# A decode layer on one NeuronCore: the order of the first loads, the cut of the last one, and the block around the programs

Three small edits were made at once to a kernel that is already bound by its loads. The last 64 rows of the q weights are loaded before the other 512. The block that wrapped the programs of the five engines is gone. The last chunk of `W_down` arrives in four pieces of 3, 3, 2 and 1 rows instead of three of 6, 2 and 1.

## Chip, cores and metric

The kernel runs on one core of a Trainium2 chip. The metric is the device time of one execution in microseconds (us). Each execution also has a *span*: the time from the first to the last instruction that the trace shows.

## The reference

It is one transformer layer at decode time (batch 4, one token, width 576):

```python
h  = x + attention(layernorm(x))      # 32 heads, 16 kv heads, head size 128, last 4096 cache positions
h2 = h + mlp(layernorm(h))            # relu(x W_gate) * (x W_up), then W_down [4608, 576]
```

The cache window and the weights are some 160 MB in bf16, each byte used once.

## The kernel before

The kernel writes lists of operations, one list per engine, with dependencies by name. `emit` turns these into semaphore waits. The parts that the change touches, cut:

```python
    def emit(self, nc, es):
        # ... number the operations, make the semaphores ...
        block = es.enter_context(nc.Block())
        def run(engine, e):
            # ... for each operation: wait for its dependencies, issue it, signal ...
        for e in ENGS:
            getattr(block, e)(lambda engine, e=e: run(engine, e))
```

In the trace of this kernel, at the line that closes the block, SyncE branches at 378.2 us, and all five engines drain and meet in a barrier whose semaphore records run from 378.39 to the end of the span at 378.58.

All large loads go through SyncE's queue, in order: q weights, then K and V tiles of 4 MB through four slots, then `A_wo`, `W_gate`, `W_up` and `W_down`:

```python
        place(("wq", 0), wq_off, TILE, "QMM", ...)        # 512 rows, 128 x 32 KB
        P.dma("sync", ("L", "wq", 1), ...)                # 64 rows, 128 x 4 KB
        # ... K and V tiles, then the other weights ...
        for j in range(4):                                # W_down: 4 chunks of 9 rows per partition
            for r0, r1 in ((0, 9),) if j < 3 else ((0, 6), (6, 8), (8, 9)):
                place(("wd", j, r0), ...)
```

The last stage multiplies each row of `W_down` (two matmuls, `n` = 0 and 1) as its piece lands. Then both halves are copied out of PSUM, the output is stored, and SyncE waits for the store to land:

```python
        for j in range(4):
            for r in range(9):
                for n in range(2):
                    if n == 0:
                        if r == 0 or (j == 3 and r in (6, 8)):
                            deps.append(("L", "wd", j, r))
                    pe(("DOWN", n), ...)
        # ... two copies, two stores ...
        P.op("sync", None, None, [("O", n) for n in range(2)])
```

## Time and profile before

| what | value |
|---|---|
| time before the prediction, 3 runs | median 380.56 us (379.36 to 380.57) |
| time of the profiled run, and its span | 380.66 us, 378.58 us |
| bytes loaded, mean rate over the span | 159.7 MB, 422 GB/s |

Four lines of the page of the kernel before follow: PE and the other engines with busy time, share and instruction count; the DMA engines' busy tenths in 40 slices of the span; and the chain of work that ended last, by engine and by line.

```profile
PE 213.2 (56%) x1471; PEld 37.6 (10%) x703; DVE 225.6 (60%) x164; ACT 54.4 (14%) x85; POOL 10.6 (3%) x29
...
DMA  8999999999999999999999999999999999999994
...
DMA 56%; PE 22%; DVE 20%; issue 0%; SPq 0%; ACT 0%
DMA sb_arena<-in_A_k_cache_dram 48%; DVE sb_arena L427 16%; PE psb L34 13%; DMA sb_arena<-in_B_W_down_dram 8%; PE psb L451 4%; PE psb L512 3%; DVE sb_o_tmp L525 1%; DVE sb_pp L490 1%; PE psb L707 1%; PE psb L478 1%; DVE sb_pp L473 0%; DVE sb_hx L456 0%; ACT sb_pp L470 0%; SPq L286 0%; DVE sb_out_sb L710 0%
```

The DMA engines are busy from the second slice to the last but one, and no compute engine is busy more than 60%. The chain is mostly waits for loads. So only the two ends can be gained from, unless the rate changes.

The end of the chain of waits, in order of time (start, duration, what):

```profile
341.77 32.17 DMA sb_arena<-in_B_W_down_dram
373.94 0.04 issue
373.98 2.39 PE psb L707 x18
376.37 0.43 DVE sb_out_sb L710
```

The timeline of the same stretch shows start, duration, engine, line, operation and shape; in brackets stand the idle time before and what ended it:

```profile
371.93 1.28 PE L707 MATMUL psb<-sb_arena,sb_pp 128*32 128x288 bf16 x18 [1.83 <-DMA sb_arena<-in_B_W_down_dram]
...
373.98 2.35 PE L707 MATMUL psb<-sb_arena,sb_pp 128*32 128x288 bf16 x18 [0.77 <-DMA sb_arena<-in_B_W_down_dram]
376.36 0.45 DVE L710 CAST sb_out_sb<-psb 32x288 bf16<-32x288 f32 x1 [10.68 <-PE psb L707]
```

And the same stretch by windows: length, busy time of PE, PEld (weight loads), DVE, ACT and POOL with instructions in brackets, then the granted PE clock (1.00 is full speed), the DMA share and GB/s:

```profile
371.00:373.30 2.30, 1.28 (x18) 0.82 (x18) 0.00 (x0) 0.00 (x0) 0.00 (x0) 1.00 0.82 333
373.30:374.00 0.70, 0.02 (x2) 0.02 (x4) 0.00 (x0) 0.00 (x0) 0.00 (x0) 0.54 0.46 171
374.00:375.00 1.00, 1.00 (x10) 0.67 (x12) 0.00 (x0) 0.00 (x0) 0.00 (x0) 0.50 0.08 30
375.00:376.40 1.40, 1.33 (x12) 0.54 (x8) 0.04 (x1) 0.01 (x1) 0.00 (x0) 0.50 0.00 0
```

Each of the two matmul groups has 18 matmuls of the same shape. The first took 1.28 us, the second 2.35 us. The window view gives the reason: the clock granted to PE is 1.00 up to 373.3 and 0.50 from 374 on.

The end of the execution, by line: what SyncE's sequencer did on the block's closing line (its count, minimum, median and maximum in ns, first and last start in us):

```profile
L136 SPq COMPARE_BRANCH  x1: 33/33/33, 378.2 to 378.2; - x1
L136 SPq DRAIN  x1: 7/7/7, 378.4 to 378.4; - x1
L136 SPq EVENT_SEMAPHORE  x1: 17/17/17, 378.5 to 378.5; - x1
```

The output had landed at 378.18 by the record of landings. The branch, the drain and the barrier that follow end the span at 378.58.

### The profile page before, as it was taken

The numbers are of one execution on the slowest core, as the hardware profiler recorded it, in microseconds if no ns is written. First come the engines' busy times: TensorE is split into PE (matmuls) and PEld (weight loads), VectorE is DVE, ScalarE is ACT, GpSimd is POOL, SyncE is SP. The second block draws the span as 40 slices with busy tenths as digits, with TensorE's granted clock in tenths as the row PEclk, the third lists the DMA queues.
The fourth block names the chain that finished last, engine by engine and source line by source line (L and its number), as shares of the span: only waits on it lengthen the run. The fifth ranks groups of instructions, "written<-read, shape, count | busy, mean of one in ns | idle before, by whom it ended". The sixth has DMA issues, their size and how long they took to land.

```text
span 378.6 us, 2587 instructions
## 1 busy us (share of the span) xinstructions
PE 213.2 (56%) x1471; PEld 37.6 (10%) x703; DVE 225.6 (60%) x164; ACT 54.4 (14%) x85; POOL 10.6 (3%) x29
## 2 busy tenths in 40 slices
PE   0404442239919091749292835573746697885764
PEld 0000000001001010101010100010100011002422
DVE  3178878779392959593848777666658513334120
ACT  3192000211010114010101140101010501113010
POOL 8200000000000000000000000000000000000000
PEclk9966866659969788697888796989686978998697
DMA  8999999999999999999999999999999999999994
GB/s 333 440 443 429 409 435 443 443 429 409 435 443 440 427 414 433 443 436 426 419 435 443 429 426 426 435 433 436 429 422 435 436 429 429 448 413 421 418 423 183
DMA packets 6659, 159.74 MB, mean 422 GB/s; under 512 B 749, under 2 KB 889, under 8 KB 1529
## 3 DMA queue, kind: packets, MB, share of 16 engines
q1 hardware_dynamic: 6632, 159.59, 98.3%
q8 instruction: 8, 0.13, 0.1%
q14 instruction: 3, 0.02, 0.0%
q10 hardware_dynamic: 16, 0.01, 0.0%
HBM read 159.58 MB, written 0.00 MB: 422 GB/s over the span
## 4 chain that ended last, share of the span: by engine, by line
DMA 56%; PE 22%; DVE 20%; issue 0%; SPq 0%; ACT 0%
DMA sb_arena<-in_A_k_cache_dram 48%; DVE sb_arena L427 16%; PE psb L34 13%; DMA sb_arena<-in_B_W_down_dram 8%; PE psb L451 4%; PE psb L512 3%; DVE sb_o_tmp L525 1%; DVE sb_pp L490 1%; PE psb L707 1%; PE psb L478 1%; DVE sb_pp L473 0%; DVE sb_hx L456 0%; ACT sb_pp L470 0%; SPq L286 0%; DVE sb_out_sb L710 0%
## 5 line engine op out<-in xcount | busy, mean ns | idle before, releaser
L427 DVE STREAM_TRANSPOSE sb_arena<-sb_arena 128x8192 f32<-128x8192 f32 (+1 forms) x19 | 139.9, 7365 | 67.5 <-DMA sb_arena<-in_A_k_cache_dram 67.5
L451 PE MATMUL psb<-sb_arena 128*32 128x512 bf16 x256 | 41.8, 627 | 120.3 <-DVE sb_arena L427 120.3
L34 PE MATMUL psb<-sb_arena,sb_pp 128*128 128x512 bf16 x384 | 108.3, 392 | 0.0
L512 PE MATMUL psb<-sb_arena,sb_pp 128*128 128x512 bf16 x128 | 50.9, 398 | 8.9 <-DVE sb_o_tmp L525 8.9
L522 ACT COPY sb_o_tmp<-psb 32x512 f32<-32x512 f32 x32 | 18.5, 578 | 181.4 <-PE psb L34 181.1
L34 PE MATMUL psb<-sb_arena 128*32 128x512 bf16 x256 | 43.4, 645 | 0.0
L525 DVE TENSOR_TENSOR sb_o_tmp<-psb,sb_fm 32x512 f32<-32x512 f32 x32 | 21.7, 678 | 18.6 <-PE psb L34 18.1
L451 PEld LDWEIGHTS psb<-sb_arena 128*32 128x32 bf16 x256 | 9.1, 119 | 162.9 <-DVE sb_arena L427 133.3
L512 PEld LDWEIGHTS psb<-sb_arena,sb_pp 128*128 128x128 bf16 x128 | 12.8, 100 | 116.6 <-issue 116.6
L529 DVE TENSOR_REDUCE sb_o_sel<-sb_o_tmp 128x128 f32<-128x512 f32 x16 | 17.7, 1105 | 0.5
L470 ACT ACTIVATE sb_pp<-psb,sb_hx 128x1024 bf16<-128x1024 f32 x4 | 4.5, 1114 | 80.7 <-DVE sb_hx L467 80.7
L490 DVE TENSOR_TENSOR sb_pp<-psb,sb_m 128x1024 bf16<-128x1024 f32 x8 | 9.3, 1207 | 4.8 <-PE psb L478 4.8
L485 ACT ACTIVATE sb_pp<-psb,sb_m 128x512 bf16<-128x512 f32 x16 | 9.7, 693 | 14.9 <-PE psb L478 14.9
L528 DVE TENSOR_TENSOR sb_o_tmp<-sb_o_tmp,sb_fm 64x512 f32<-64x512 f32 x16 | 11.0, 689 | 0.5
L418 ACT COPY sb_arena<-sb_q_keep 32x256 bf16<-32x256 bf16 x8 | 9.7, 1449 | 0.1
L707 PE MATMUL psb<-sb_arena,sb_pp 128*32 128x288 bf16 x72 | 6.2, 327 | 4.0 <-DMA sb_arena<-in_B_W_down_dram 4.0
L473 DVE STREAM_TRANSPOSE sb_pp<-sb_pp 128x1024 bf16<-128x1024 bf16 x4 | 5.0, 1245 | 5.1 <-ACT sb_pp L470 5.1
L478 PE MATMUL psb<-sb_pp,sb_to_v 128*32 128x256 bf16 x64 | 4.3, 401 | 6.3 <-DVE sb_pp L473 6.3
L404 DVE CAST sb_pp<-psb 128x512 bf16<-128x512 f32 x1 | 2.4, 2427 | 8.8 <-PE psb L384 8.8
L710 DVE CAST sb_out_sb<-psb 32x288 bf16<-32x288 f32 x1 | 0.4, 446 | 10.7 <-PE psb L707 10.7
L34 PE MATMUL psb<-sb_arena,sb_hnT 128*32 128x384 bf16 x80 | 6.4, 405 | 0.0
L456 DVE TENSOR_REDUCE sb_hx<-psb 128x1 f32<-128x1024 f32 x4 | 4.9, 1225 | 2.0 <-PE psb L34 2.0
(123 smaller groups left out, 81.2 us busy)
## 6 DMA issues: line engine op xcount, KB each, us to landing
sb_arena<-in_A_k_cache_dram SPq DMA_DIRECT2D x16, 4096.0 KB, 26.2
sb_arena<-in_A_v_cache_dram SPq DMA_DIRECT2D x16, 4096.0 KB, 28.5
sb_arena<-in_A_wo_dram SPq DMA_DIRECT2D x1, 4608.0 KB, 25.0
sb_arena<-in_B_W_gate_dram SPq DMA_DIRECT2D x1, 4608.0 KB, 26.5
sb_arena<-in_A_wq_dram SPq DMA_DIRECT2D x1, 4096.0 KB, 12.4
sb_arena<-in_B_W_down_dram SPq DMA_DIRECT2D x3, 1296.0 KB, 30.6
sb_arena<-in_B_W_up_dram SPq DMA_DIRECT2D x1, 3456.0 KB, 27.5
sb_arena<-in_B_W_up_dram SPq DMA_DIRECT2D x1, 1152.0 KB, 29.9
```

The costliest lines, as they stand in the source:

```text
L34: return e.add_instruction(mybir.InstMatmult(name=e.bass.get_next_instruction_name(), engine=mybir.EngineType.PE, ins=[e.lower_ap(rhs), e. ...
L418: act("QW", lambda e, i=i, q=q: e.copy(out=bass.AP(tensor=arena, offset=32 * i * AW + 2 * i + q, ap=[[AW, 32], [512, 16], [136, 4], [32, 4]]),
L427: dve(("TRA", g), lambda e: e.transpose(out=dst, in_=src), [("L", "K", g)] if lo == 0 else [])
L451: fn = lambda e, out_=out_, lhsT=lhsT, rhs=rhs, start=start, stop=stop: e.matmul(out_, lhsT=lhsT, rhs=rhs, start=start, stop=stop, skip_gr ...
L485: act(("EV", b, 0), lambda e, a=a: e.activation(out=bass.AP(tensor=pp, offset=2 * a, ap=[[PPW, 128], [8, 2], [32, 128], [1, 2]]), in_=bank ...
L490: dve(("EV", b, 1), lambda e, n=n: e.tensor_tensor(out=bass.AP(tensor=pp, offset=16 + 8 * n, ap=[[PPW, 128], [32, 128], [2, 4], [1, 2]]), ...
L512: fn = lambda e, lhsT=lhsT, rhs=rhs, k=k, j=j: e.matmul(bank[2 + j], lhsT=lhsT, rhs=rhs, start=(k == 0), stop=(k == 7), skip_group_check=True)
L522: act(("OSC", g), lambda e, j=j: e.copy(out=o_tmp[32 * j:32 * j + 32, 0:512], in_=bank[2 + j][32 * j:32 * j + 32, :]), [("PV", g), ("OSEL" ...
L525: dve(("OSD", g), lambda e, j=j: e.tensor_tensor(out=ot(32 * j, 32), in0=bank[2 + j][32 * j:32 * j + 32, :].rearrange("p (t d) -> p t d", ...
L528: dve(("OS", g), lambda e: e.tensor_tensor(out=ot(64, 64), in0=ot(64, 64), in1=fmb(64, 64), op=ALU.mult), [("OSC", g)])
L529: dve(("OSEL", g), lambda e: e.tensor_reduce(out=o_sel[:, qd, b, :], in_=o_tmp[:, 0:512].rearrange("p (t d) -> p d t", d=DH), axis=AX.X, o ...
L707: pe(("DOWN", n), lambda e, j=j, r=r, n=n, wv=wv: e.matmul(bank[n][32 * n:32 * n + 32, 0:288], lhsT=hhT[:, r * 128 + 32 * j:r * 128 + 32 * ...
```

## The change

The intent: SyncE's first load becomes the short one, the branches and the closing barrier go away, and PE has less to do after the last large piece has landed. Where the text speaks of 4 KB or 32 KB runs, it means the contiguous bytes that a load brings to one partition, not runs of the kernel.

```diff
-        block = es.enter_context(nc.Block())
-
@@
         for e in ENGS:
-            getattr(block, e)(lambda engine, e=e: run(engine, e))
+            run(getattr(nc, e), e)
@@
+        P.dma("sync", ("L", "wq", 1), lambda e: e.dma_start(out=pT[:, 0:2048], in_=last_rows(A_wq)), "d_wq1")
         s = ring_slot()
         wq_off = slot0 + s * TILE
         place(("wq", 0), wq_off, TILE, "QMM", ...)
-        P.dma("sync", ("L", "wq", 1), lambda e: e.dma_start(out=pT[:, 0:2048], in_=last_rows(A_wq)), "d_wq1")
@@
-            for r0, r1 in ((0, 9),) if j < 3 else ((0, 6), (6, 8), (8, 9)):
+            for r0, r1 in ((0, 9),) if j < 3 else ((0, 3), (3, 6), (6, 8), (8, 9)):
@@
-                        if r == 0 or (j == 3 and r in (6, 8)):
+                        if r == 0 or (j == 3 and r in (3, 6, 8)):
```

## The prediction

> **What bounds the kernel now.** One stream of loads. The page's slice table shows the DMA engines at 9 tenths from the second slice to the last but one, 422 GB/s over the span (159.7 MB, 378.6 us). The chain that ended last is 56% DMA; in order of time it ends "341.77 32.17 DMA W_down", 2.39 us of matmuls, a 0.43 us copy. PE (56% busy) and DVE (60%) do not set the pace. Only the start and the tail after the last bytes can pay; the rate between is left alone.
>
> **Parts of the change.**
>
> 1. W_down in 3, 3, 2, 1. By the records of landings the piece of 6 rows lands at 373.94, the next at 374.70, the last at 375.01. The timeline shows chunk 2's 18 matmuls from 371.93 in 1.28 us (done 373.2), PE idle until 373.98, then 18 matmuls in 2.35 us: the window table grants clock 0.50 from 374 on, so a row (2 matmuls) costs 0.24 us instead of 0.13. When row 6 is reached its data is there: the tail after 373.98 is PE work, not DMA. The 6 rows landed 2.05 us after chunk 2 (371.89), so 3 rows should land near 372.95 (estimate), and PE does them in its gap, from 373.2. Rows 3 to 5 start near 374.0; rows 6 (landing about 374.8) and 8 (about 375.1) hold nothing up. Three rows fewer after 374: 0.72 us[...]: **-0.65 us**. At full clock only about -0.1: then the landing at 375.0 binds.
>
> 2. No block. After the output lands (378.18) the records show wait and branch at 378.20, a drain, and a barrier of all engines ending at 378.58: **-0.35 us** if nothing replaces it. At the start one branch per engine goes between release (0.73) and first issue (0.80): at most **-0.05**.
>
> 3. Last 64 rows of the q weights first. K tile 0 still lands at 24.21. The 4 MB part lands near 14.5 instead of 13.24; q matmuls begin 1.25 us later and the query matrix is written near 27.3 instead of 26.0. Its reader waits for the transpose of K tile 0 (24.24 + 8.72 = 32.96): 5.6 us of slack. The next K load waits for the q matmuls (issue 17.8, then 19), with loads queued to 43.6. So 0. The first packets are 4 KB instead of 32 KB; the ramp may move by ±0.2.
>
> **Sum.** -0.65 - 0.35 - 0.05 = -1.05 us on 380.56: **379.5 us**, range **378.5 to 380.6** (the runs before span 1.2 us). Faster by over 2%: 0.01; within 2%: 0.985; slower by over 2%: 0.005.
>
> **What would show it.** Of the last 18 matmuls 6 before 373.9, the last 0.65 earlier; last landing up to 0.1 later. No drain and barrier after the output lands. The q matmuls at 14.5, K tile 0's transpose still at 24.2.
>
> **What would make it wrong.** The stream's end is set by the slowest of 16 DMA engines: the last piece's completions run from 372.63 to 375.01[...]. [...] So would another clock grant in the tail.

The sum came to -1.05 us. Cut are passages that no trace or run here shows: in part 1 an allowance that took its 0.72 us to the -0.65 of the sum, and in the last paragraph a reason for the spread of the completions and one further way in which the stream's end might move. "So would another clock grant" means: it too would move the end. The "±0.2" of the ramp and "up to 0.1 later" were my allowances, not measured: later, over all profiles, K tile 0's first completion came 0.27 us earlier with the order changed, and the last landing 0.38 earlier.

## More of the kernel before

The span is shorter than the time, and the difference turns out to matter here. I call it "time minus span".

All runs quoted are of the state that the measurements call fast. Within that state a second grouping shows up: of 64 runs of the kernel before, 43 took 379.33 to 379.78 us and 21 took 380.24 to 380.73 us, with none between. I call them *usual* and *long* runs.

## The result and the profile after

In the measurement of the pair, the changed kernel took 377.88 us (median of 6 runs, 377.84 to 378.10) and the kernel before 379.69 (6 runs, 379.36 to 380.57). The ratio is 0.9948, with a 95% interval of 0.9935 to 0.9961. A ratio here is the mean time of one kernel's fast runs over that of the other's of the same rounds, so it is not quite the ratio of these medians. By the means the gain is 1.97 us (377.92 against 379.90), by usual runs 1.64 us (377.88 against 379.52, the median of all 43 usual runs; the later gains in usual runs are against this too). I had forecast 1.05.

The page after, the same lines as before:

```profile
PE 208.8 (55%) x1456; PEld 37.6 (10%) x703; DVE 226.2 (60%) x164; ACT 54.3 (14%) x85; POOL 10.5 (3%) x29
...
DMA  8999999999999999999999999999999999999996
...
DMA 56%; PE 21%; DVE 20%; issue 1%; SPq 1%; ACT 0%
DMA sb_arena<-in_A_k_cache_dram 48%; DVE sb_arena L425 16%; PE psb L34 13%; DMA sb_arena<-in_B_W_down_dram 9%; PE psb L449 4%; PE psb L510 3%; DVE sb_o_tmp L523 1%; DVE sb_pp L488 1%; PE psb L476 1%; SPq L284 0%; DVE sb_pp L471 0%; DVE sb_hx L454 0%; ACT sb_pp L468 0%; PE psb L705 0%; DVE sb_out_sb L708 0%
```

The shares are the same: the kernel is still one stream of loads. The end of the chain, the timeline, the windows, and the line on which SyncE now ends, as before:

```profile
341.69 32.31 DMA sb_arena<-in_B_W_down_dram
374.00 0.04 issue
374.04 0.70 PE psb L705 x6
374.74 0.43 DVE sb_out_sb L708
```

```profile
371.23 1.65 PE L705 MATMUL psb<-sb_arena,sb_pp 128*32 128x288 bf16 x24 [1.82 <-DMA sb_arena<-in_B_W_down_dram]
...
373.33 0.55 PE L705 MATMUL psb<-sb_arena,sb_pp 128*32 128x288 bf16 x6 [0.46 <-DMA sb_arena<-in_B_W_down_dram]
...
374.04 0.66 PE L705 MATMUL psb<-sb_arena,sb_pp 128*32 128x288 bf16 x6 [0.17 <-DMA sb_arena<-in_B_W_down_dram]
374.73 0.45 DVE L708 CAST sb_out_sb<-psb 32x288 bf16<-32x288 f32 x1 [9.73 <-PE psb L705]
```

```profile
371.00:373.30 2.30, 1.65 (x24) 1.09 (x24) 0.00 (x0) 0.00 (x0) 0.00 (x0) 1.00 0.87 345
373.30:374.00 0.70, 0.55 (x6) 0.21 (x6) 0.00 (x0) 0.00 (x0) 0.00 (x0) 1.00 0.42 152
374.00:375.00 1.00, 0.66 (x6) 0.21 (x6) 0.27 (x1) 0.24 (x1) 0.00 (x0) 1.00 0.00 0
375.00:376.40 1.40, 0.00 (x0) 0.00 (x0) 0.18 (x1) 0.15 (x1) 0.00 (x0) 1.00 0.01 3
```

```profile
L110 SPq EVENT_SEMAPHORE  x1: 17/17/17, 376.6 to 376.6; - x1
```

The group at 371.23 holds 24 matmuls: the 18 of chunk 2 and the 6 of rows 0 to 2 of the last chunk, done in PE's former gap. Rows 3 to 5 follow at 373.33, and the last six matmuls at 374.04, each piece's as it lands. The clock is 1.00 throughout. After the output's landing (376.55) there is one wait of SyncE and nothing else. The output's own way, from the copy to its landing, is unchanged (1.82 us in both).

Part by part, the two profiles and times differ so (before, after):

| term | before | after | difference |
|---|---|---|---|
| last piece of `W_down` landed | 375.01 | 374.35 | -0.66 |
| from there to the start of the copy (376.36, 374.73) | 1.35 | 0.38 | -0.97 |
| output landed to end of span | 0.40 | 0.03 | -0.37 |
| time minus span | 2.08 | 1.28 | -0.80 |

The last row is not in the span at all, so no view of the profile shows it. The sum is -2.8 us, more than the gain by means or by usual runs: the profiled run of before, at 380.66, was a long one. These four terms are what the experiments had to sort out.

### The profile page after: what moved, and what is told of

The parts are those of the page before. It is cut to its first block, busy times and chain, and to the rows that moved or that the text cites. A ratio compares the mean times of both kernels' runs of the same rounds, so it can differ in the third digit from the quotient of the medians.

```text
span 376.6 us, 2562 instructions
## 1 busy us (share of the span) xinstructions
PE 208.8 (55%) x1456; PEld 37.6 (10%) x703; DVE 226.2 (60%) x164; ACT 54.3 (14%) x85; POOL 10.5 (3%) x29
## 4 chain that ended last, share of the span: by engine, by line
DMA 56%; PE 21%; DVE 20%; issue 1%; SPq 1%; ACT 0%
DMA sb_arena<-in_A_k_cache_dram 48%; DVE sb_arena L425 16%; PE psb L34 13%; DMA sb_arena<-in_B_W_down_dram 9%; PE psb L449 4%; PE psb L510 3%; DVE sb_o_tmp L523 1%; DVE sb_pp L488 1%; PE psb L476 1%; SPq L284 0%; DVE sb_pp L471 0%; DVE sb_hx L454 0%; ACT sb_pp L468 0%; PE psb L705 0%; DVE sb_out_sb L708 0%
## 5 line engine op out<-in xcount | busy, mean ns | idle before, releaser
L449 PE MATMUL psb<-sb_arena 128*32 128x512 bf16 x256 | 44.5, 640 | 118.8 <-DVE sb_arena L425 118.8
L34 PE MATMUL psb<-sb_arena,sb_pp 128*128 128x512 bf16 x382 | 107.3, 389 | 2.9 <-issue 2.8
L510 PE MATMUL psb<-sb_arena,sb_pp 128*128 128x512 bf16 x115 | 44.8, 389 | 8.9 <-DVE sb_o_tmp L523 8.9
L34 PE MATMUL psb<-sb_arena 128*32 128x512 bf16 x256 | 45.4, 645 | 0.0
L705 PE MATMUL psb<-sb_arena,sb_pp 128*32 128x288 bf16 x72 | 5.4, 288 | 3.8 <-DMA sb_arena<-in_B_W_down_dram 3.8
```

Source lines behind the costliest of these rows:

```text
L34: return e.add_instruction(mybir.InstMatmult(name=e.bass.get_next_instruction_name(), engine=mybir.EngineType.PE, ins=[e.lower_ap(rhs), e. ...
L449: fn = lambda e, out_=out_, lhsT=lhsT, rhs=rhs, start=start, stop=stop: e.matmul(out_, lhsT=lhsT, rhs=rhs, start=start, stop=stop, skip_gr ...
L510: fn = lambda e, lhsT=lhsT, rhs=rhs, k=k, j=j: e.matmul(bank[2 + j], lhsT=lhsT, rhs=rhs, start=(k == 0), stop=(k == 7), skip_group_check=True)
```

## The experiments

All kernels gave results that the comparison with the reference accepted. The runs of the kernel before on the same chip serve for the ratio of each.

### The kernel before again

No edit.

> The kernel before, unchanged, as the noise floor and as a second profile of it. Every theory: ratio 1.000, within 0.1%. Open is how far its profiled span and its tail repeat: the profile of before has 378.58 us of span in 380.66 us (2.08 us outside the span), the changed kernel 376.59 in 377.87 (1.28 outside). Theory A (the block costs time outside the span): about 2.1 us outside again, whatever the span. Theory C (the clock granted in the tail was luck): the last 18 matmuls take between 1.0 and 2.4 us from run to run and the span moves with them by up to 1 us.

Measured: 379.51 us (379.38 to 379.61, 5 runs, all usual), ratio 0.9986 (0.9972 to 1.0000); time minus span 2.11 (median). Nothing was changed, yet the ratio is 0.14% off, more than I had expected: 6 of the 11 runs that it compares with were long. A ratio this close to 1 says little, so I go by usual runs below. Its profile has the span 377.46. The timeline of its tail, and one window:

```profile
371.78 1.28 PE L707 MATMUL psb<-sb_arena,sb_pp 128*32 128x288 bf16 x18 [1.82 <-DMA sb_arena<-in_B_W_down_dram]
...
373.84 1.37 PE L707 MATMUL psb<-sb_arena,sb_pp 128*32 128x288 bf16 x18 [0.78 <-DMA sb_arena<-in_B_W_down_dram]
375.25 0.45 DVE L710 CAST sb_out_sb<-psb 32x288 bf16<-32x288 f32 x1 [9.68 <-PE psb L707]
```

```profile
374.00:375.00 1.00, 1.00 (x18) 0.60 (x14) 0.00 (x0) 0.00 (x0) 0.00 (x0) 1.00 0.07 24
```

The same 18 matmuls take 1.37 us here, at clock 1.00. The last piece landed at 374.87 and the last matmul began at 374.91: the tail of a usual run ends with the landing, not with PE. The profile that I had predicted from was a long run with a half-clock tail. Of the 20 profiles taken, only three have half clock while the last chunk is multiplied: that of this one long run, and those of the two kernels below that leave out matmuls on purpose. In the long run the clock fell at 373.36 although no gap of PE between the `W_down` groups before it was longer than 1.83 us; what made it fall there was not shown. What is outside the span repeats at 2.1 us.

### Only the block removed

```diff
-        block = es.enter_context(nc.Block())
-            getattr(block, e)(lambda engine, e=e: run(engine, e))
+            run(getattr(nc, e), e)
```

> Only the block removed. Theory A (the block costs 0.36 us of barrier at the end of the span and some 0.8 us more outside the span, where I counted nothing): -1.15 us, time minus span falls from about 2.1 to 1.3. Theory B (the surplus came from an earlier end of the load stream, by the order of the q weights): -0.4 us, time minus span unchanged. Theory C (the surplus came from the clock in the tail): -0.4 us too.

Measured: 378.23 us (four usual runs at 378.17 to 378.25, two long at 379.02 and 379.38), ratio 0.9961 (0.9945 to 0.9976). Time minus span fell to 1.28. The gain in usual runs is 1.33 us: 0.8 outside the span and 0.37 after the output's landing. The other 0.15 is not told apart from the spread of the stream's end between profiles. Theory A held, B and C missed by 0.9.

### Only the split

```diff
-((0, 6), (6, 8), (8, 9))
+((0, 3), (3, 6), (6, 8), (8, 9))
```

> Only the last W_down chunk in 3, 3, 2, 1. My prediction: -0.65 us where the tail runs at half clock, -0.1 where it runs at full clock. Theory A: -0.1 to -0.65, all of it in the span. Theory C (earlier work keeps the clock up in the tail): -1.0 us, and the last group of matmuls runs at full clock in the profile. Time minus span stays at 2.1 in all.

Measured: 379.52 us (five usual runs at 379.44 to 379.77, one long at 380.54), ratio 0.9992 (0.9977 to 1.0006). The tail in the profile:

```profile
373.75 0.55 PE L707 MATMUL psb<-sb_arena,sb_pp 128*32 128x288 bf16 x6 [0.47 <-DMA sb_arena<-in_B_W_down_dram]
...
374.46 0.66 PE L707 MATMUL psb<-sb_arena,sb_pp 128*32 128x288 bf16 x6 [0.16 <-DMA sb_arena<-in_B_W_down_dram]
```

Rows 3 to 5 and the last six matmuls wait for their pieces; the last piece landed at 374.77 and the last matmul began at 374.82. PE waits less and starts earlier, and nothing is gained: the last landing sets the end either way. My -0.65 us is not there in usual runs.

### Only the order of the q weights

```diff
+        P.dma("sync", ("L", "wq", 1), ...)      # the 64 rows, 4 KB runs
         place(("wq", 0), ...)                   # the 512 rows, 32 KB runs
-        P.dma("sync", ("L", "wq", 1), ...)
```

> Only the last 64 rows of the q weights first. Theory A and my prediction: 0, within 0.2 us. Theory B (the order changes which DMA engine is the slowest, and the end of the stream): -0.6 us, the last landing at 374.4 instead of 375.0, K tile 0 lands 0.2 earlier.

Measured: 379.12 us (five usual runs at 379.04 to 379.15, one long at 380.11), ratio 0.9981 (0.9965 to 0.9997). The gain in usual runs is 0.4 us, where I had counted 0. K tile 0 landed at 23.90 and the last piece at 374.47, so the stream ends earlier, much as theory B has it, by two thirds of the size it asked for.

### No block, but a barrier at the end

```diff
         for e in ENGS:
             run(getattr(nc, e), e)
+        nc.all_engine_barrier()
```

> The block removed, but an all-engine barrier put back at the end by hand, so the barrier without the branches and without the separate bodies. Theory A1 (the barrier at the end holds every engine until the output has landed[...]): time minus span back at 2.1 us, time back at 379.3 to 379.5 in the usual runs. Theory A2 (the branches cost it): time minus span stays at 1.27, time about 378.6 (the 0.36 us of barrier come back inside the span alone).

Measured: 379.30 us (usual runs 379.24 to 379.55, one long at 380.31), ratio 0.9994 (0.9980 to 1.0008); time minus span 2.06. SyncE's end, by the barrier's line:

```profile
L119 SPq DRAIN  x1: 7/7/7, 377.0 to 377.0; - x1
L119 SPq EVENT_SEMAPHORE  x1: 17/17/17, 377.1 to 377.1; - x1
```

The barrier alone brings back the 0.8 us outside the span, and 0.29 us inside it (0.40 with the block). So it is the barrier that costs, not the branches, of which about 0.1 us is seen at the end. What follows the last instruction is outside the trace, so why time minus span is 0.8 us longer after a barrier was not shown.

### The main q weights still first, cut so that the first load has 4 KB runs

```diff
-        place(("wq", 0), wq_off, TILE, ...)
+        for lo, hi in ((0, 2048), (2048, TILE)):
+            place(("wq", 0, lo), wq_off + lo, hi - lo, ...)   # 128 x 4 KB, then 128 x 28 KB
```

> The kernel before, with the main q weights still first but cut in two loads: the first of runs of 4 KB a partition (0.5 MB), the second of 28 KB. Theory R (the gain of the order is the ramp of the stream: short first packets start the 16 engines sooner): as in the order experiment, K tile 0's first completion near 23.3 instead of 23.55, usual runs 0.2 to 0.4 us faster than before (379.1 to 379.3). Rival (it matters that the last 64 rows come first, or it was chance): no change, 379.5 in the usual runs, first completion 23.5.

Measured: 379.20 us (five usual runs at 379.14 to 379.25, one long at 380.30), ratio 0.9990 (0.9977 to 1.0004). The usual runs gained 0.33 us, as theory R had it, so it is not the last 64 rows that matter. Both first loads that gained have 4 KB runs and are also small as a whole (0.5 MB against 4 MB); no run here tells the two apart. K tile 0's first completion came at 23.44, between the two expectations, so how the 0.33 comes about is only partly shown. Over all profiles the picture is this (means, us; "first" and "last" of the 16 completions of a load):

| profiles | K tile 0 first | K tile 0 last | last `W_down` piece first | last |
|---|---|---|---|---|
| 32 KB runs first (12 profiles) | 23.54 | 24.04 | 372.80 | 374.81 |
| 64 rows first, 4 KB runs (6 profiles) | 23.27 | 23.93 | 372.56 | 374.43 |
| main weights cut, 4 KB runs first (1 profile) | 23.44 | 23.92 | 372.68 | 374.52 |

With the 64 rows first the first completion is 0.27 us earlier from the start on, and 0.24 at the end. The rest of the 0.38 at the end is a smaller distance between the first and the last of the 16 completions (1.87 against 2.01 us). The lead arises in the first 4 us: by then the packets of the six profiles with the 64 rows first had moved 0.64 to 0.70 MB, those of the twelve 0.54 to 0.59, and of the cut weights 0.62 (each packet's bytes spread over its duration). At 370 us the six are still ahead, by 0.09 MB in the mean, which is 0.2 us at 430 GB/s (an estimate; between the first and the last, the slices of the page of before run at 409 to 448).

### The tail's PE work doubled, with 6, 2, 1 rows and with 3, 3, 2, 1

```diff
+                    if j == 3:
+                        pe(None, ...)   # the same matmul into an unused bank, ahead of the real one
                     pe(("DOWN", n), ...)
```

> The kernel before, pieces of 6, 2 and 1 rows, with each matmul of the last chunk done twice, once into an unused bank: the PE work of the tail doubled, as half clock would. Theory P (the split pays only where PE, not the landing, ends the tail): last matmul starts at about 376.0 at full clock, 1.1 us after that of the unchanged kernel, time 380.6 in the usual runs.

> The same doubling with pieces of 3, 3, 2 and 1. Theory P: rows 0 to 2 are done in the gap before 373.7, the last matmul starts near 375.2, and the kernel is 0.75 us faster than the doubled one of 6, 2 and 1 rows; without doubling the same split was worth nothing (379.52 against 379.51). If the split is worth nothing here either, the reason I gave for it is wrong altogether.

Measured: 6, 2, 1 rows: two usual runs at 380.39 and 380.79, two long at 381.93 and 382.06. 3, 3, 2, 1 rows: 380.03 us (379.82 to 380.10, 4 runs). The first and the last pair of matmuls of the last chunk in the timelines, first of 6, 2, 1, then of 3, 3, 2, 1:

```profile
373.71 0.30 PE L708 MATMUL psb<-sb_arena,sb_pp 128*32 128x288 bf16 x2 [0.77 <-DMA sb_arena<-in_B_W_down_dram]
...
375.80 0.29 PE L712 MATMUL psb<-sb_arena,sb_pp 128*32 128x288 bf16 x2
```

```profile
372.86 0.29 PE L708 MATMUL psb<-sb_arena,sb_pp 128*32 128x288 bf16 x2
...
375.22 0.29 PE L712 MATMUL psb<-sb_arena,sb_pp 128*32 128x288 bf16 x2
```

With doubled work PE is what ends the tail, and the split is worth 0.58 us (375.80 to 375.22) at full clock; usual runs differ by 0.56 (380.59, the middle of two runs 0.4 apart, against 380.03). So the reason I gave for the split is right where PE is late, and only there. The expected 0.75 was too much, because the tail of 6, 2, 1 rows ended 0.2 us earlier than I had worked out.

### The changed kernel without the split, and the changed kernel again

```diff
-((0, 3), (3, 6), (6, 8), (8, 9))
+((0, 6), (6, 8), (8, 9))
```

> The changed kernel with the last chunk again in 6, 2 and 1 rows (no block, order changed). Theory: the split is worth 0.1 us at most in a usual run, so 377.9 to 378.0 in the usual runs, as the changed kernel; but a run whose tail falls into half clock is about 1 us longer (378.9), in perhaps one of three. Rival (the split gives its 0.65 us in company of the others): 378.5 in the usual runs.

> The changed kernel again, on this chip and in the same rounds, to compare with. 377.9 in the usual runs, time minus span 1.26. If the split guards against the longer runs there are none, or shorter ones (at most 0.5 us over the usual); if not, one or two of six near 378.9, as the split alone had one of six at 380.54 against 379.47.

Measured: without the split 378.00 us (377.79 to 378.07 in four runs, one at 378.32, one long at 378.96), ratio 0.9956; the changed kernel 377.91 us (377.80 to 377.98, 5 runs, none long), ratio 0.9950. Usual runs are equal to 0.1 us, and the last landing is too (374.30 and 374.39).

### Extra matmuls while PE waits for `W_down`

```diff
+                for k in range({(0, 8): 12, (1, 8): 12, (3, 2): 4}.get((j, r), 0)):
+                    pe(None, ...)       # into an unused bank
```

On the changed kernel (as shown) and on the kernel before (12, 12 and 8 after chunks 0, 1 and 2):

> The changed kernel with extra matmuls into an unused bank while PE waits for the next W_down chunk (12 after chunk 0, 12 after chunk 1, 4 after rows 0 to 2 of the last). Theory H (the longer runs are those in which PE's idle gaps in the last 8 us let the granted clock fall to half in the tail): all runs 377.8 to 378.0, none near 378.9. If the longer runs have another cause, they stay as frequent.

> The kernel before with such extra matmuls (12, 12 and 8 after chunks 0, 1 and 2). So far 11 of 33 runs of the kernel before were near 380.5 instead of 379.5. Theory H: none or hardly any here, usual runs unchanged at 379.5, ratio about 0.999. If the longer runs have another cause: about two of six near 380.5.

Measured: 378.02 us (377.79 to 378.23, 6 runs, none long) and 379.54 us (379.31 to 379.68, 6 runs, none long), ratios 0.9953 and 0.9993. No usual run became faster. The second was run again, with the split alone, to count long runs:

> The kernel before with extra matmuls once more, to count longer runs: theory H none or one of six near 380.5, chance about two. Usual runs 379.3 to 379.7.

> The split alone once more, to count longer runs: if it guards against them, none or one of six near 380.5; if the count so far is chance, about two of six. Usual runs 379.45 to 379.55.

Measured: 379.46 us (379.27 to 379.62, 5 runs, none long) and 379.52 us (four usual runs at 379.49 to 379.58, one long at 380.39), ratios 0.9996 and 1.0003.

The kernel before with extra matmuls has thus 0 long runs of 11, the unchanged one 21 of 64. If each run were an independent draw, none of 11 would come up about once in 80 times ((43/64) to the 11th). The runs of one job may not be independent, so this supports theory H without settling it.

### PE left idle before the last chunk, with both splits

The matmuls of `W_down` chunks 0 to 2 are left out and their loads kept. Their outputs are wrong, which doesn't matter for the times. The comparison with the reference passed nonetheless, so it is not sharp enough to see three quarters of this sum; it says little about this stage.

```diff
-        for j in range(4):
+        for j in (3,):
```

> Wrong result on purpose: the kernel before without the matmuls of W_down chunks 0 to 2 (their loads stay), so that PE idles from 366 to 373.8 and the clock should have fallen when the last chunk, in 6, 2 and 1 rows, comes. Theory H (idle PE, half clock, PE-bound tail): the profile shows the last 18 matmuls at 0.24 us a pair, the last one starts near 375.9, and nearly all runs are long: 380.5.

> Wrong result on purpose: the same with 3, 3, 2 and 1 rows. My prediction's step for half clock: last matmul near 375.2, 0.65 to 0.75 us faster than the cold kernel of 6, 2 and 1 rows, 379.8. If both cold kernels run at full clock in the profile, theory H has fallen.

Measured: 380.52 us (380.48 to 380.65, 4 runs) and 379.76 us (379.70 to 379.89, 4 runs). Windows and timeline of the first, then the timeline of the second:

```profile
366.00:369.00 3.00, 0.07 (x2) 0.00 (x0) 0.00 (x0) 0.00 (x0) 0.00 (x0) 1.00 1.03 435
369.00:372.00 3.00, 0.00 (x0) 0.00 (x0) 0.00 (x0) 0.00 (x0) 0.00 (x0) 0.54 0.97 407
...
373.50:375.00 1.50, 1.19 (x12) 0.75 (x14) 0.00 (x0) 0.00 (x0) 0.00 (x0) 0.50 0.22 81
```

```profile
373.81 2.34 PE L707 MATMUL psb<-sb_arena,sb_pp 128*32 128x288 bf16 x18 [7.74 <-DMA sb_arena<-in_B_W_down_dram]
376.19 0.45 DVE L710 CAST sb_out_sb<-psb 32x288 bf16<-32x288 f32 x1 [10.68 <-PE psb L707]
```

```profile
372.89 0.90 PE L707 MATMUL psb<-sb_arena,sb_pp 128*32 128x288 bf16 x6 [6.75 <-DMA sb_arena<-in_B_W_down_dram]
...
373.94 1.63 PE L707 MATMUL psb<-sb_arena,sb_pp 128*32 128x288 bf16 x12 [0.15 <-DMA sb_arena<-in_B_W_down_dram]
375.60 0.45 DVE L710 CAST sb_out_sb<-psb 32x288 bf16<-32x288 f32 x1 [10.03 <-PE psb L707]
```

PE idles, the granted clock falls to 0.50 within the window from 369 to 372, and the 18 matmuls take 2.34 us, as in the first profile of before. Every run is now as long as the long runs of the kernel before (21 runs, median 380.50). With the finer pieces 6 matmuls are done before 373.9, the copy starts at 375.60 instead of 376.19, and the kernel is 0.76 us faster. That is my prediction's step for half clock, at its size. Here it applied with the clock at 0.50 before the last chunk came and no other matmuls waiting. Two runs with the split alone were long all the same (380.54 and 380.39); neither was profiled. If their clock fell before chunk 2, its 18 matmuls would take some 2.35 us instead of 1.28, PE would work without a pause from there to the end and no split would help. That is an estimate from these two times, not shown.

### The last wait on another engine, and still shorter first runs

```diff
-        P.op("sync", None, None, [("O", n) for n in range(2)])
+        P.op("gpsimd", None, None, [("O", n) for n in range(2)])
```

```diff
-        P.dma("sync", ("L", "wq", 1), ...)      # 128 x 4 KB
+        for k in (1, 2):
+            P.dma("sync", ("L", "wq", k), ...)  # 128 x 2 KB each
```

> The changed kernel with the last wait (for the output's landing) on GpSimd, idle since 12 us, instead of SyncE. If what follows outside the span is the closing work of the engine that ends last, time minus span changes from 1.27 in either direction by some tenths; if it is a fixed cost of the launch once the last engine is done, it stays at 1.2 to 1.3 and the time at 377.9.

> The changed kernel with the last 64 rows of the q weights in two loads of 2 KB runs a partition instead of one of 4 KB. Theory R (shorter first packets, shorter ramp): K tile 0's first completion at 23.1 to 23.2 instead of 23.2 and at most 0.1 us gained: 377.8. If one more issue of 0.4 us leaves a gap in the stream instead, up to 0.3 us lost.

Measured: 378.53 us with the wait on GpSimd (378.36 to 378.60, 6 runs); time minus span 1.79 instead of 1.27. The span (376.8) is as before. GpSimd's only closing instruction:

```profile
L110 POOLq EVENT_SEMAPHORE  x1: 17/17/17, 376.8 to 376.8; - x1
```

So here what follows differed with what ended last: 2.1 us after a barrier of all, 1.79 after GpSimd, 1.27 after SyncE. SyncE was the better choice.

With 2 KB runs: 380.27 us (379.37 to 380.69, 6 runs), 2.4 us slower than the changed kernel. The direction of the second expectation came true at eight times its size. One window of this kernel, then of the changed one:

```profile
4.00:6.00 2.00, 0.00 (x0) 0.00 (x0) 1.57 (x4) 1.56 (x2) 2.00 (x4) 1.00 0.67 197
```

```profile
4.00:6.00 2.00, 0.00 (x0) 0.00 (x0) 1.56 (x5) 0.90 (x2) 2.00 (x4) 1.00 0.80 332
```

From 4 to 6 us the stream moved 197 GB/s against 332, and K tile 0 landed at 26.21 instead of 24.04. The bytes missing by 8 us (1.78 MB moved against 2.35, each packet's bytes spread over its duration: 0.57 MB, 1.3 us at 430 GB/s) explain a part of it, and the stream never makes them up: 0.58 MB are missing at 370 us. The last of K tile 0's 16 completions was also further behind the first, by 1.92 us against 0.81. Why the large packets started so late and unevenly is open, and so is which of the two changes did it, the shorter runs or the additional load: no run has one without the other.

No version beat the changed kernel.

## Why the prediction was wrong

It forecast 379.5 us, at the earliest 378.5; measured was 377.88. That the change stays within 2% was right; its size was not. The starting point was off as well: 380.56 us is a long run, and the kernel before in its usual runs (379.52) already stands where the forecast put the changed one. From 379.52 the same terms give 378.47, so of the miss of 1.6 us about 1.0 is the base. The rest is two gains that were missing, less one that did not exist and so hid a part of them.

1. **"No block ... -0.35 us if nothing replaces it", -0.05 at the start.** The mechanism was right and the term mis-sized. The 0.40 us after the output's landing went to 0.03, but the same barrier costs 0.8 us more outside the span. Removing the block is worth 1.33 us in usual runs. The start gained nothing that the profiles show: SyncE's first issue is at 0.80 with the block and without, and neither trace has a record of a branch there. The hint was in the given data: the time was 380.66 and the span 378.58. I treated the 2.08 us as fixed.
2. **"W_down in 3, 3, 2, 1 ... -0.65 us".** This step failed. It was read off one profile, of a long run, with the clock at 0.50 in the tail. In the usual runs that were profiled the clock is 1.00 there, the last landing sets the end, and the split is worth nothing (379.52, the median of nine usual runs with it, against 379.52; 377.93 without it in the changed kernel against 377.91 with it). I had written the right alternative, "At full clock only about -0.1", and put the wrong one into the sum, although two of the three times (380.56, 380.57) were near that of the profile and one (379.36) was not. With half clock forced by idling PE the step holds: 0.76 us.
3. **"Last 64 rows of the q weights first ... So 0", "K tile 0 still lands at 24.21".** The slack argument was right: the q matmuls began at 14.37 instead of 13.28 and nothing waited. The stream's start was mis-sized: a small first load of short runs brings 0.4 us (0.33 in the other form), carried to the last landing. I had allowed for ±0.2.
4. **"Last landing up to 0.1 later".** It came 0.66 earlier in these two profiles; between groups of profiles the order explains 0.38 of it, and the rest is spread between runs.

In usual runs the parts alone give -1.33 (block), 0.00 (split) and -0.40 (order), together -1.73 us, against -1.64 measured for all three. The surplus of the means (-1.97) is the long runs: 2 of 6 of before, none of the changed kernel. Whether the split makes long runs rarer stays open. Without it 27 of 93 runs were long (21 of 64 of the kernel before, and 6 of 29 with only the block, the order, or both changed, the barrier moved, or the first load cut). With it, and without extra matmuls, 2 of 28 were long (0 of 17 of the changed kernel, once and again, and with the wait moved; 2 of 11 of the split alone; the 2 KB variant, whose times scatter, and the kernels with doubled or left-out matmuls are not counted).

## What to carry to other kernels

Compare the measured time with the profile's span before costing anything: here the closing barrier cost 0.8 us outside the span and 0.37 inside it, and dropping it, which only the end of the kernel needed, gave 1.33 us, more than the reordering (0.40). When run times fall into two groups, find out which group the profile belongs to before reading a tail from it; here finer last pieces paid where PE was late (0.56 us with doubled work, 0.76 at half clock) and brought 0.00 in usual runs, where the last landing set the end. And here the stream of loads got going sooner with a small load of 4 KB runs ahead of the large ones (0.33 to 0.40 us gained), while two such loads of 2 KB runs let it run thin (197 GB/s against 332 from 4 to 6 us, 2.4 us lost).
